# Attention weights used three steps late, and queries and keys of six batches transposed by DMA, in a fused top-k attention and MLP kernel

## The chip, the cores and the metric

The kernel runs on one core of a Trainium2 chip. The metric is the device time of one execution in microseconds; of the kernel before, three runs gave 1605.85, 1606.17 and 1606.31 us, a median of 1606.17 us. The engines are named as the profile names them: PE (TensorE, with PEld for its weight loads), DVE (VectorE), ACT (ScalarE), POOL (GpSimd) and SP (SyncE, which here issues every DMA).

## What is computed

```python
# q, k, v: (8 batches, 8 heads, 576 rows, 64), float32
scores = matmul(q, k^T) / 8
kth    = the 32nd largest score of each row
scores = where(scores >= kth, scores, -1e9)
attn   = exp(scores - rowmax); attn /= (rowsum + 1e-9)
x      = matmul(attn, v), heads side by side: (4608 tokens, 512)
h      = x @ w_in                       # 512 -> 2048
g      = h where h >= 1; 0 where h <= -1; (h + 1)^2 / 4 between
out    = g @ w_out                      # 2048 -> 512
```

## The kernel before

**Steps.** The attention is cut into 144 steps. A step takes 128 query rows against all 576 keys for a pair of heads: four head pairs for each of the four 128-row blocks of a batch, and two steps for the 64 rows that are left over (in these one step serves four heads). Batches go in pairs: 16 steps of the even batch, two and two leftover steps of both, 16 steps of the odd one, so 36 steps a pair. A block of query rows is called a round.

**One step on each engine.** PE multiplies queries and keys (`scores`, tile `sp`, L285), ACT copies the result out (`s`, L287). DVE finds the 32 largest scores (L300 to L386; its first instruction that needs `s` of the next step is L300, tile `more`), ACT takes the exponential (L323), DVE masks and sums (L386), POOL divides (L339). `move_w` (L412) brings the weights into the layout that PE needs without using PE: ACT splits each 32-bit word into its two 16-bit halves (`halves`, L416), SP writes them to DRAM (`rows`, L418), waits, and issues a DMA transpose into `wT` (L419). `values` (L425) then multiplies by V (tile `po`) and ACT copies the product into `xT` (L446). After the last head pair of a block, `mlp` (L457) queues that block's two matrix products, in pieces: eight `ph` groups (L466) and sixteen `py` products (L489), with ACT and POOL between them (L470 to L484).

**Queries and keys** also need a transpose. Before, PE does it against an identity matrix: `queries_of` (L259, tile `pq`, L264) and `keys_of` (L221, tiles `pk` L240 and `pkt` L248), and ACT copies the result out of PSUM (L266, L244, L253). A batch takes 16 + 4 key transposes and 16 + 4 query transposes. The PSUM tiles of `pq`, `pk`, `pkt` and `sp` share one pair of buffers (tag `a`).

**The order** on PE, DVE, ACT and POOL is written out by hand (`manual_schedule`, L580). The loop over steps m (L661) has seven slots; the pieces of DVE's work of step m are given out over the slots, and at the end of each slot `advance` (L562) lets PE take as much queued MLP work as an even share allows (L669 to L673). Within step m, before:

- slot 1: query transposes for step m+3, and in even steps a piece of the next batch's keys
- slot 2: `move_w` of step m-1
- slot 4: scores of step m+2, then `values` of step m-2

SP's order is left to the framework, which sorts it by dependencies. Each of these queues runs strictly in order. For the first steps, until the weights of the MLP have been converted (the variable `early`), another order holds, with transposes of the weights on PE (`transpose_w`).

Of the kernel before, what the change touches and what calls it, by code (L numbers as in the profile page):

```python
# [10 lines left out]
F32 = mybir.dt.float32  # L11
U16 = mybir.dt.uint16
U32 = mybir.dt.uint32
I32 = mybir.dt.int32
AF = mybir.ActivationFunctionType
# [9 lines left out]
def kernel(  # L25
# [10 lines left out]
    nc = tc.nc  # L36
    B, H, S, D = q.shape
    NTOK, DM = out.shape
    DFF = moe_w_in.shape[1]
    P = 128  # L40
# [3 lines left out]
    NHP = H // 2  # L44
    NT = S // P
    SM = NT * P
    TL = S - SM
    assert 2 * TL == P
    SH = S // 2
    BLOCKS = 2 * NT + 1  # L50
# [18 lines left out]
    tiny = const.tile([P, 2], F32, name="tiny")  # L69
# [50 lines left out]
    def load(pool, i, bufs=3):  # L120
        if i < n_pieces and i not in loaded:
            if room and i < 28:
                loaded[i] = room[i % 8]
            else:
                loaded[i] = pool.tile([P, 2 * WC], U32, name="raw", bufs=bufs)
            nc.sync.dma_start(out=loaded[i], in_=pieces_of_weights[i][1].bitcast(U32))

    def words_of(pool, i, bufs=3):
        load(pool, i, bufs)
        words = loaded.pop(i).rearrange("p (n t) -> p n t", t=2)  # L130
        return words[:, :, 0], words[:, :, 1]
# [30 lines left out]

    def inspect_piece(pool, i):

        _, hi = words_of(pool, i, 2)
        for x in range(2):
            sign = pool.tile([P, WC], F32, name="sign", bufs=1)
            nc.scalar.activation(sign, hi.bitcast(F32), AF.Sign, bias=tiny[:, x:x + 1],  # L168
                                 accum_out=signs[:, x, i:i + 1])


    def run(ctx, paired):
# [7 lines left out]
        def whole(x, b):  # L180

            return x[b, :, 0:SM, :].rearrange("h (p c) d -> p h c d", c=NT)
# [38 lines left out]
        def keys_of(b):  # L221
# [14 lines left out]
            for hp in range(NHP):  # L236
# [19 lines left out]
                    got["v"], got["v_tl"] = load_values(b)  # L256
                yield got

        def queries_of(q_in, t, copy=nc.scalar.copy):  # L259
            n = P if t < NT else TL  # L260
            qT = stage.tile([P, NHP, n], F32, name="qT" if t < NT else "qTt")
            pt = ps.tile([P, NHP, n], F32, name="pq", tag="a", bufs=2)
            for hp in range(NHP):
                nc.tensor.transpose(pt[:, hp, :], q_in[:, 2 * hp:2 * hp + 2].rearrange("p j d -> p (j d)"),  # L264
                                    ident[0:n, 0:n])
            copy(qT, pt)  # L266
            return qT
# [62 lines left out]
        def divide(st):  # L330
            rz = att.tile([P, 2], F32, name="rz")
            nc.vector.reciprocal(rz, st["z"])
            if st["by_tensor"]:
                st["rz"] = diag = (late or words).tile([P, 2, P], F32, name="diag", bufs=1)
                for i in range(2):
                    nc.scalar.activation(diag[:, i, :], ident, AF.Copy, scale=rz[:, i:i + 1])
            else:
                for i in range(2):
                    nc.gpsimd.tensor_scalar(st["e"][:, i, :], st["e"][:, i, :], rz[:, i:i + 1], 1.0, ALU.mult, ALU.mult)  # L339
            if paired:  # L340
                m, seconds, kth = st["m"], st["seconds"], st["kth"]
                nc.gpsimd.tensor_tensor(out=excess[:, 2 * m:2 * m + 2], in0=seconds[:, 8:9 + SPLIT:SPLIT], in1=kth[:, LAST:7:-SPLIT],
                                        op=ALU.subtract)
# [50 lines left out]

        def transpose_w(st):
            w = st["e"]
            st["wT"] = wT = (late or words).tile([P, BLOCKS, P], F32, name="wT", bufs=2 if late else 1)
            pt = ps.tile([P, 2, NT, P], F32, name="pw", tag="a", bufs=2)
            for i in range(2):
                for c in range(NT):  # L400
                    nc.tensor.matmul(pt[:, i, c, :], w[:, i, main(i)][:, c * P:(c + 1) * P], st["rz"][:, i, :],  # L401
                                     start=True, stop=True)
            for i in range(2):
                nc.scalar.copy(wT[:, i * (NT + 1):i * (NT + 1) + NT], pt[:, i])
            pt = ps.tile([P, P], F32, name="pwt", tag="a", bufs=2)
            for i in range(2):
                nc.tensor.matmul(pt[i * TL:(i + 1) * TL, :], w[:, i, tail(i)], st["rz"][:, i, :], start=True, stop=True)
            nc.scalar.copy(wT[:, NT], pt)
# [1 line left out]


        def move_w(st):  # L412
            st["wT"] = wT = late.tile([P, BLOCKS, P], F32, name="wT", bufs=2)
            halves = late.tile([P, 2, 2 * S], U16, name="halves")
            for i in range(2):
                nc.scalar.copy(halves[:, :, i * S:(i + 1) * S], st["e"][:, i, :].bitcast(U16).rearrange("p (k t) -> p t k", t=2))  # L416
            rows = dram.tile([P, 2, 2 * S], U16, name="rows")
            nc.sync.dma_start(out=rows, in_=halves)  # L418
            nc.sync.dma_start_transpose(wT.bitcast(U16), rows.rearrange("p t k -> (p t) k"))  # L419
# [37 lines left out]
        def mlp(xT, rows, pool, last):  # L457
# [28 lines left out]
            def final(f):  # L486
                if f == 0:
                    py.append(ps.tile([P, DM], F32, name="py", tag="py", bufs=1))
                nc.tensor.matmul(py[0], gs[f // group][:, f % group], w_out[:, f, :], start=(f == 0), stop=(f == NF - 1))  # L489
                if f == NF - 1:  # L490
                    y = (late or words).tile([P, DM], F32, name="y", bufs=2)
                    nc.scalar.copy(y, py[0])  # L492
                    for p0, p1, dst in rows:
                        nc.sync.dma_start(out=dst, in_=y[p0:p1])
# [111 lines left out]
        def queries(m):  # L606
            nonlocal pe_time
            if m < n and steps[m][0:2] not in qTs:
                r = steps[m][0:2]
                qTs[r] = queries_of(q_ins[r], r[1], nc.vector.tensor_copy if m == 0 else nc.scalar.copy)  # L610
                fetch(rounds.index(r) + 2)
                pe_time += 0.5

        def begin(m):
            b, t, hp, ch, col = steps[m]
# [45 lines left out]
        for m in range(n + 2):  # L661
# [6 lines left out]

            share, left = (total - spent) / (n + 2 - m), sum(x[0] for x in pending)  # L669
            for r in sorted(ready):  # L670
                if r + 3 > m and r >= valued:
                    share = min(share, left / (r + 3 - m))
                    left += NK * NF + NF * DM // P  # L673
            top_k, parts = None, [0] * SLOTS
            if m < n:
# [7 lines left out]
            for slot in range(SLOTS):  # L683
                now = start + (dve_time - start) * (slot + 1) / SLOTS
                for _ in range(parts[slot]):
                    next(top_k, None)
                if m < n and converted < n_pieces:
                    if slot in now_converting:
                        convert(now)
                elif slot == 3 and late is not None:  # L690
                    if m % 2:
                        inspect()
                    elif paired:
                        load(late, inspected, 2)
                if slot == 1 and 1 <= m <= n and state[m - 1]["by_tensor"]:
                    pe_time = max(pe_time, done[m - 1] + 2.0) + 1.0
                    transpose_w(state[m - 1])
                    ready_at[m - 1] = pe_time + 1.8
                if slot == 2 and 1 <= m <= n and not state[m - 1]["by_tensor"]:
                    move_w(state[m - 1])  # L700
                    ready_at[m - 1] = done[m - 1] + 14.0
                if slot == 2 and m == n and paired:
                    judge(ps, att)
                if slot == 2 and (early or m == first_late or m >= n - 1):
                    values_until(m)
                if m == 0 and slot in (1, 2):
                    next(first)
                if slot == 4:
                    begin_at(m + 2)
                    if not early:  # L710
                        values_until(m - 1)
                if slot == (6 if early else 1):
                    queries(m + 3)
                    if m < n and prep is None and next_keys < B and steps[m][0] == next_keys - 1 and steps[m][1] >= 1:
                        prep = keys_of(next_keys)
                    if prep is not None and m % 2 == 0:
                        got = next(prep, None)
                        pe_time += 0.5
                        if got is None:
                            prep, next_keys = None, next_keys + 1  # L720
                        else:
                            keys[next_keys] = got
                advance((EARLY_SHARE if early else share) / SLOTS if m < n else 32.0, now)
# [52 lines left out]
```

## Time and profile before

| quantity | before |
|---|---|
| median of three runs | 1606.17 us |
| the profiled execution's own time | 1610.32 us |
| its span | 1608.5 us |
| DVE busy / ACT busy / POOL busy | 1422.1 / 1140.4 / 943.3 us |
| share of the 16 DMA engines' time taken by SP's queue | 51.8% |
| bytes read from and written to DRAM | 62.91 and 86.11 MB |

Busy time is summed per engine; an engine that is not the bottleneck may idle for free. In a group of instructions the columns are: line, engine, operation, output and inputs, shapes, count, then busy time in us and mean ns of one, then idle time of the engine just before them and what ended it. A row of waits reads: who waited, for whom, us in total, times, longest. The durations of pipelined matmuls overlap: what one costs is the distance from its start to the start of the next.

### The profile page before, as it was taken

The numbers are of one execution on the slowest core, as the hardware profiler recorded it, in microseconds if no ns is written. First come the engines' busy times: TensorE is split into PE (matmuls) and PEld (weight loads), VectorE is DVE, ScalarE is ACT, GpSimd is POOL, SyncE is SP. The second block draws the span as 40 slices with busy tenths as digits, with TensorE's granted clock in tenths as the row PEclk, the third lists the DMA queues.
The fourth block names the chain that finished last, engine by engine and source line by source line (L and its number), as shares of the span: only waits on it lengthen the run. The fifth ranks groups of instructions, "written<-read, shape, count | busy, mean of one in ns | idle before, by whom it ended". The sixth has DMA issues, their size and how long they took to land.

```text
span 1608.5 us, 32395 instructions
## 1 busy us (share of the span) xinstructions
PE 1514.0 (94%) x10925; PEld 1080.7 (67%) x10925; DVE 1422.1 (88%) x4443; ACT 1140.4 (71%) x2308; POOL 943.3 (59%) x1376
## 2 busy tenths in 40 slices
PE   5587999999999999999999999999999999999988
PEld 4465676777667776777667767766666667666665
DVE  7999889999998998999999998999898998889932
ACT  5677567777777767777768877776677776677632
POOL 5766466666555665655556666555555665556640
PEclk7798999999999999999999999999999999999999
DMA  9433246565465556665565545655565555544410
GB/s 252 132 96 110 72 130 174 157 158 153 133 174 161 154 143 173 161 150 145 145 172 159 160 133 157 172 143 140 135 174 146 142 142 130 145 131 126 123 51 16
DMA packets 439056, 227.92 MB, mean 142 GB/s; under 512 B 393056, under 2 KB 401248, under 8 KB 438880
## 3 DMA queue, kind: packets, MB, share of 16 engines
q1 hardware_dynamic: 438880, 225.75, 51.8%
q8 instruction: 88, 1.44, 0.4%
q14 instruction: 88, 0.72, 0.1%
HBM read 62.91 MB, written 86.11 MB: 93 GB/s over the span
## 4 chain that ended last, share of the span: by engine, by line
PE 71%; ACT 13%; POOL 4%; DVE 4%; DMA 4%; issue 3%; SPq 1%; POOLq 0%; ACTq 0%; DVEq 0%
PE ph L466 27%; PE py L489 24%; PE sp L285 8%; PE po L433 7%; ACT halves L416 3%; ACT e L323 3%; DMA wT<-rows 2%; ACT s L287 2%; ACT sign L168 2%; PE pw L401 1%; POOL e L339 1%; POOL r L483 1%; PE po L441 1%; ACT r L470 1%; POOL g L484 1%
## 5 line engine op out<-in xcount | busy, mean ns | idle before, releaser
L466 PEld LDWEIGHTS ph<-xT,w_in 128*128 128x128 f32 x4608 | 554.4, 192 | 118.3 <-issue 79.8
L466 PE MATMUL ph<-xT,w_in 128*128 128x128 f32 x4608 | 576.1, 278 | 14.8 <-ACT xT L446 12.9
L489 PE MATMUL py<-w_out,g 128*128 128x512 f32 x1152 | 558.6, 601 | 7.3 <-ACT y L492 7.1
L482 POOL TENSOR_SCALAR r<-r 128x256 f32<-128x256 f32 x276 | 150.7, 546 | 526.5 <-ACT r L470 526.1
L307 DVE MATCH_REPLACE8 more<-tops,more 128x288 f32<-128x288 f32 x864 | 375.2, 437 | 0.0
L416 ACT COPY halves<-e 128x1152 uint16<-128x1152 uint16 x260 | 288.0, 1153 | 112.7 <-POOL e L339 111.5
L470 ACT ACTIVATE r<-ph,half 128x256 f32<-128x256 f32 (+1 forms) x296 | 139.0, 470 | 241.1 <-PE ph L466 227.9
L489 PEld LDWEIGHTS py<-w_out,g 128*128 128x128 f32 x1152 | 193.5, 191 | 137.0 <-issue 131.2
L386 DVE SCALAR_TENSOR_TENSOR e<-s,kth,e 128x577 f32<-128x577 f32 x288 | 249.2, 900 | 0.1
L484 POOL TENSOR_TENSOR g<-r,g 128x256 f32<-128x256 f32 x280 | 219.6, 784 | 22.0
L323 ACT ACTIVATE e<-s,nmax 128x576 f32<-128x576 f32 x288 | 217.4, 770 | 4.7
L339 POOL TENSOR_SCALAR e<-e,rz 128x576 f32<-128x576 f32 x260 | 218.6, 851 | 0.0
L483 POOL TENSOR_TENSOR r<-r 128x256 f32<-128x256 f32 x276 | 201.5, 730 | 23.0
L300 DVE TENSOR_TENSOR more<-s 128x576 f32<-128x576 f32 x144 | 114.9, 798 | 109.0 <-ACT s L287 108.6
L287 ACT ACTIVATE s<-sp 128x576 f32<-128x576 f32 x288 | 169.2, 638 | 4.5 <-PE sp L285 4.2
L285 PE MATMUL sp<-kT,qT 64*128 64x288 f32 x1024 | 162.0, 433 | 9.9 <-ACT kT L244 9.0
L285 PEld LDWEIGHTS sp<-kT,qT 64*128 64x128 f32 x1024 | 89.6, 188 | 98.9 <-issue 29.1
L433 PE MATMUL po<-wT,v_in 128*64 128x128 f32 x2048 | 145.9, 282 | 10.3 <-DMA wT<-rows 7.9
L433 PEld LDWEIGHTS po<-wT,v_in 128*64 128x64 f32 x2048 | 113.4, 139 | 60.5 <-issue 37.5
L477 ACT ACTIVATE g<-ph,minus 128x256 f32<-128x256 f32 x280 | 131.8, 471 | 0.0
L348 DVE MAX8 tops<-more 128x8 f32<-128x288 f32 x288 | 125.4, 442 | 0.0
L300 DVE TENSOR_TENSOR less<-s 128x576 f32<-128x576 f32 x144 | 117.4, 815 | 0.0
(92 smaller groups left out, 1528.2 us busy)
## 6 DMA issues: line engine op xcount, KB each, us to landing
rows<-halves SPq DMA_DIRECT2D x130, 576.0 KB, 2.8
raw<-in_moe_w_out_dram SPq DMA_DIRECT2D x52, 256.0 KB, 2.8
raw<-in_moe_w_in_dram SPq DMA_DIRECT2D x48, 256.0 KB, 2.9
k_in<-in_k_dram SPq DMA_DIRECT2D x64, 128.0 KB, 3.2
q_in<-in_q_dram SPq DMA_DIRECT2D x32, 256.0 KB, 3.3
v_in<-in_v_dram SPq DMA_DIRECT2D x8, 1024.0 KB, 5.9
out_dram<-y SPq DMA_DIRECT2D x32, 256.0 KB, 3.0
kT<-in_moe_w_in_dram SPq DMA_DIRECT2D x16, 256.0 KB, 4.6
```

The lines of the kernel that those rows point to most:

```text
L285: nc.tensor.matmul(o[:, a0 - c0:a1 - c0], qT[d, g, :], kT[d, g, k0:k0 + a1 - a0], start=True, stop=True)
L300: nc.vector.tensor_tensor(out=x, in0=s[:, :, 0:SH], in1=s[:, :, SH:S], op=op)
L307: nc.vector.match_replace(out=st["rest"][:, i, :], in_to_replace=eight(st["tops"], i, r - 8), in_values=src[:, i, :], imm_value=LOWEST)
L323: nc.scalar.activation(e[:, i, :], s[:, i, :], AF.Exp, bias=nmax[:, i:i + 1])
L339: nc.gpsimd.tensor_scalar(st["e"][:, i, :], st["e"][:, i, :], rz[:, i:i + 1], 1.0, ALU.mult, ALU.mult)
L386: nc.vector.scalar_tensor_tensor(out=st["all"][1][:, i, :], in0=st["all"][0][:, i, :], scalar=last[i], in1=st["all"][1][:, i, :], op0=ALU. ...
L416: nc.scalar.copy(halves[:, :, i * S:(i + 1) * S], st["e"][:, i, :].bitcast(U16).rearrange("p (k t) -> p t k", t=2))
L433: nc.tensor.matmul(po[j * D:(j + 1) * D], v_in[:, h, c, :] if c < NT else v_tl[0][:, h, :], wT[:, block(j, c)], start=(c == 0), stop=(c == ...
L466: nc.tensor.matmul(ph[:, i], w_in[:, kk, f * P:(f + 1) * P], xT[:, kk], start=(kk == 0), stop=(kk == NK - 1))
L483: nc.gpsimd.tensor_tensor(out=r, in0=r, in1=r, op=ALU.mult)
L484: nc.gpsimd.tensor_tensor(out=g, in0=r, in1=g, op=ALU.add)
L489: nc.tensor.matmul(py[0], gs[f // group][:, f % group], w_out[:, f, :], start=(f == 0), stop=(f == NF - 1))
```

## The change

- `values` runs for step m-3 instead of m-2, in slot 2 instead of slot 4, ahead of the scores of step m+2, which also move from slot 4 to slot 2. `move_w` goes from slot 2 to slot 3. `wT` gets a third buffer; `advance` counts with the later supply of MLP work (`r + 4`).
- Queries and keys of batches 3 to 8 are no longer transposed by PE. `turn` does with them what `move_w` does with the weights: an ACT copy into 16-bit halves, a DMA to DRAM, a DMA transpose. For this the keys are loaded in blocks of 128 rows of all heads (`load_block`, with three DMAs a block) and not by head pair. Slots stay as they were; the last two blocks of a batch's keys (c = 3 and 4) are turned in the same slot. The buffer `parts` of the halves exists once.
- To make room, the tile for the MLP's output `y` and the buffer of the weights' inspection (`raw`) go from two to one, and `diag` shares a tag with `halves`.

```diff
+        def turn(x, dst):
+            n = x.shape[0]
+            parts = stage.tile([P, 2, H * D], U16, name="parts", tag="k_tl", bufs=1)[0:n]
+            nc.scalar.copy(parts, x.rearrange("p h d -> p (h d)").bitcast(U16).rearrange("p (k t) -> p t k", t=2))
+            lines = dram.tile([P, 2, H * D], U16, name="lines")[0:n]
+            nc.sync.dma_start(out=lines, in_=parts)
+            nc.sync.dma_start_transpose(dst.bitcast(U16), lines.rearrange("p t k -> (p t) k"))
+
+        def turned_keys_of(b):
...
+            blocks = {0: load_block(0)}
+            yield got
+            for c in range(NT + 1):
+                if c < NT:
+                    blocks[c + 1] = load_block(c + 1)
+                n = P if c < NT else TL
+                turn(blocks.pop(c)[0:n], kT[:, :, c * P:c * P + n])
+                if c == NT - 2:
+                    got["v"], got["v_tl"] = load_values(b)
+                if c != NT - 1:
+                    yield got
+
+        def turned_queries_of(q_in, t):
+            n = P if t < NT else TL
+            qT = stage.tile([P, NHP, n], F32, name="qT" if t < NT else "qTt")
+            turn(q_in, qT)
+            return qT
...
-            st["wT"] = wT = late.tile([P, BLOCKS, P], F32, name="wT", bufs=2)
+            st["wT"] = wT = late.tile([P, BLOCKS, P], F32, name="wT", bufs=3)
...
-                    y = (late or words).tile([P, DM], F32, name="y", bufs=2)
+                    y = (late or words).tile([P, DM], F32, name="y", bufs=1)
...
-                qTs[r] = queries_of(q_ins[r], r[1], nc.vector.tensor_copy if m == 0 else nc.scalar.copy)
+                if r[0] > 1:
+                    qTs[r] = turned_queries_of(q_ins[r], r[1])
+                else:
+                    qTs[r] = queries_of(q_ins[r], r[1], nc.vector.tensor_copy if m == 0 else nc.scalar.copy)
+                    pe_time += 0.5
                 fetch(rounds.index(r) + 2)
-                pe_time += 0.5
...
-                if r + 3 > m and r >= valued:
-                    share = min(share, left / (r + 3 - m))
+                if r + 4 > m and r >= valued:
+                    share = min(share, left / (r + 4 - m))
...
-                if slot == 2 and 1 <= m <= n and not state[m - 1]["by_tensor"]:
+                if slot == 3 and 1 <= m <= n and state[m - 1] is not None and not state[m - 1]["by_tensor"]:
                     move_w(state[m - 1])
-                    ready_at[m - 1] = done[m - 1] + 14.0
+                    ready_at[m - 1] = done[m - 1] + 15.0
...
-                if slot == 4:
+                if slot == 2 and not early:
+                    values_until(m - 2)
+                if slot == (4 if early else 2):
                     begin_at(m + 2)
-                    if not early:
-                        values_until(m - 1)
...
-                        prep = keys_of(next_keys)
+                        prep = (turned_keys_of if next_keys > 1 else keys_of)(next_keys)
```

More of the change, by code (lines that the diff above doesn't have):

```diff
@@ L163, in inspect_piece @@
     def inspect_piece(pool, i):
-        _, hi = words_of(pool, i, 2)
+        lo, hi = words_of(pool, i, 1)
         for x in range(2):
-            sign = pool.tile([P, WC], F32, name="sign", bufs=1)
-            nc.scalar.activation(sign, hi.bitcast(F32), AF.Sign, bias=tiny[:, x:x + 1],
+            nc.scalar.activation(lo.bitcast(F32), hi.bitcast(F32), AF.Sign, bias=tiny[:, x:x + 1],
                                  accum_out=signs[:, x, i:i + 1])
@@ L257, in keys_of, with load_block @@
                 yield got
+        def turn(x, dst):
[6 more added lines that the diff above has]
+        def turned_keys_of(b):
+            kT = stage.tile([P, NHP, S], F32, name="kT")
+            got = dict(kT=kT)
+            def load_block(c):
+                x = stage.tile([P, H, D], F32, name="k_block", tag="k_in")
+                ends = k[b, :, SM:S, :].rearrange("h p d -> p h d")
+                if c < NT:
+                    nc.sync.dma_start(out=x[:, 0::2, :], in_=whole(k, b)[:, 0::2, c, :])
+                    nc.sync.dma_start(out=x[TL:P, 1::2, :], in_=whole(k, b)[0:P - TL, 1::2, c, :])
+                else:
+                    nc.sync.dma_start(out=x[0:TL, 0::2, :], in_=ends[:, 0::2, :])
+                nc.sync.dma_start(out=x[0:TL, 1::2, :], in_=whole(k, b)[P - TL:P, 1::2, c - 1, :] if c else ends[:, 1::2, :])
+                return x
+            blocks = {0: load_block(0)}
+            yield got
+            for c in range(NT + 1):
+                if c < NT:
+                    blocks[c + 1] = load_block(c + 1)
[10 more added lines that the diff above has]
+            return qT
         def queries_of(q_in, t, copy=nc.scalar.copy):
@@ L333, in divide @@
             if st["by_tensor"]:
-                st["rz"] = diag = (late or words).tile([P, 2, P], F32, name="diag", bufs=1)
+                st["rz"] = diag = (late or words).tile([P, 2, P], F32, name="diag", tag="halves", bufs=1)
                 for i in range(2):
@@ L396, in transpose_w @@
             w = st["e"]
-            st["wT"] = wT = (late or words).tile([P, BLOCKS, P], F32, name="wT", bufs=2 if late else 1)
+            st["wT"] = wT = (late or words).tile([P, BLOCKS, P], F32, name="wT", bufs=3 if late else 1)
             pt = ps.tile([P, 2, NT, P], F32, name="pw", tag="a", bufs=2)
@@ L609, in queries @@
                 r = steps[m][0:2]
-                qTs[r] = queries_of(q_ins[r], r[1], nc.vector.tensor_copy if m == 0 else nc.scalar.copy)
+                if r[0] > 1:
+                    qTs[r] = turned_queries_of(q_ins[r], r[1])
+                else:
+                    qTs[r] = queries_of(q_ins[r], r[1], nc.vector.tensor_copy if m == 0 else nc.scalar.copy)
+                    pe_time += 0.5
                 fetch(rounds.index(r) + 2)
-                pe_time += 0.5
         def begin(m):
@@ L693, in run @@
                     elif paired:
-                        load(late, inspected, 2)
+                        load(late, inspected, 1)
                 if slot == 1 and 1 <= m <= n and state[m - 1]["by_tensor"]:
@@ L714, in run @@
                     if m < n and prep is None and next_keys < B and steps[m][0] == next_keys - 1 and steps[m][1] >= 1:
-                        prep = keys_of(next_keys)
+                        prep = (turned_keys_of if next_keys > 1 else keys_of)(next_keys)
                     if prep is not None and m % 2 == 0:
                         got = next(prep, None)
-                        pe_time += 0.5
+                        pe_time += 0.5 if next_keys < 2 else 0.0
                         if got is None:
```

## The prediction

> **What bounds the kernel now.** I read the page's engine table and its slices first, then the busy time of the even stretch from 200 to 1500 us.
>
> ```profile
> PE 1514.0 (94%) x10925; PEld 1080.7 (67%) x10925; DVE 1422.1 (88%) x4443; ACT 1140.4 (71%) x2308; POOL 943.3 (59%) x1376
> ...
> PE   5587999999999999999999999999999999999988
> ...
> PEclk7798999999999999999999999999999999999999
> ```
>
> ```profile
> 200.00:1500.00 1300.00, 1271.45 (x9359) 901.07 (x9358) 1195.72 (x3750) 956.63 (x1883) 785.60 (x1137) 1.00 0.56 150
> ```
>
> The columns of the second are PE, PEld, DVE, ACT and POOL busy, the granted clock, the DMA share and GB/s. From 200 us on PE is busy 97.8% at full clock, DVE 92.0%. The 250 masking instructions (L386, two a step) in this stretch make 125 steps, so a step takes 10.40 us, of which DVE is busy 9.57. A busy PE may still hide slack, so I looked at its instructions in order of time, in a step that nothing disturbs and in one with a query transpose:
>
> ```profile
> 1197.39 1.24 PE L285 MATMUL sp<-kT,qT 64*128 64x288 f32 x8
> 1198.56 1.09 PE L433 MATMUL po<-wT,v_in 128*64 128x128 f32 x16
> 1199.49 0.39 PE L433 MATMUL po<-wT,v_tail 128*64 128x128 f32 x4
> 1199.81 2.05 PE L466 MATMUL ph<-xT,w_in 128*128 128x128 f32 x16
> 1201.69 1.88 PE L489 MATMUL py<-w_out,g 128*128 128x512 f32 x4
> 1203.41 1.95 PE L466 MATMUL ph<-xT,w_in 128*128 128x128 f32 x16
> 1205.20 1.88 PE L489 MATMUL py<-w_out,g 128*128 128x512 f32 x4
> 1207.01 1.24 PE L285 MATMUL sp<-kT,qT 64*128 64x288 f32 x8
> ...
> 1223.49 0.60 PE L264 MATMUL pq<-ident,q_in 128*128 128x128 f32 x4
> 1223.93 1.95 PE L466 MATMUL ph<-xT,w_in 128*128 128x128 f32 x16
> ```
>
> Each burst starts before the one ahead of it has ended: 1207.01 - 1197.39 = 9.62 us for a plain step with no gap at all. That is above DVE's 9.57. So PE bounds, by a little, and DVE follows. The waits agree: DVE stands for `s`, which PE makes, while PE stands for little:
>
> ```profile
> DVE more L300 <- ACT s L287: 108.6, 89, 4.9
> ...
> PE ph L466 <- ACT xT L446: 12.9, 10, 2.2
> ...
> PE po L433 <- DMA wT<-rows: 7.9, 6, 3.5
> ```
>
> The Trainium skill speaks against this reading: its page "Perfetto Trace Analysis", section "Identifying the Most-Contended Engine", says that matmul busy time misleads because matmuls are pipelined, and that the share of weight loading should be used. By that share (67%) PE would have a third to spare, and taking work from it would be worth nothing. The gapless starts above say otherwise, and the sum goes by them.
>
> **The change, part by part.**
>
> *Transposes off PE.* A batch has 32 of 128 columns and 8 of 64. Four of the former cost 1223.93 - 1223.49 = 0.44 us from start to start, 0.11 each; for the latter I take 0.10 at most. Six batches: 6 x (32 x 0.11 + 8 x 0.10) = 26 us off PE. The busy times of these rows give an upper bound:
>
> ```profile
> L240 PE MATMUL pk<-ident,k_in 128*128 128x128 f32 x128 | 20.7, 289 | 5.8 <-ACT s L287 5.0 <-ACT wT L404 0.8
> L264 PE MATMUL pq<-ident,q_in 128*128 128x128 f32 x128 | 19.4, 274 | 3.6 <-ACT s L287 2.8 <-DVE kT L244 0.8
> ```
>
> With 3.9 and 3.7 us for the leftover rows, 47.7 x 6/8 = 36 us; the difference is each burst's end, which lies under the next burst. The built instruction lists show the same: priced by start-to-start distances, PE's work falls by 25.5 us. **-26.**
>
> *Values one step later and ahead of the scores.* `wT` gets 5 slots (0.71 of a 10.4 us step, 7.4 us) more time. The waits of `po` for it in this stretch and its end are 7.9 (L433) and 2.1 (L441) us; one of 2.55 us at the very end stays. **-8** (0 to -10). The waits of `ph` for `xT`, 12.9 + 1.9 us, are those of a new block's first product for the last `values`; now a scores burst of 1.17 us (1197.39 to 1198.56) stands between, against a mean wait of 1.3 us. **-10** (0 to -15).
>
> *ACT.* Sixty turns add as many copies. The nearest row is `halves`:
>
> ```profile
> L416 ACT COPY halves<-e 128x1152 uint16<-128x1152 uint16 x260 | 288.0, 1153 | 112.7 <-POOL e L339 111.5
> ```
>
> 1024 of 1152 columns make 1.03 us, 62 us in all. The copies out of PSUM that go are 8 x 0.578 + 2 x 0.366 + 4 x 0.587 + 0.373 = 8.1 us a batch, 48 us. ACT gains 13 us where it idles 343 of 1300: nothing by itself. But `parts` exists once: when blocks 3 and 4 of the keys are turned in one slot, ACT's second copy waits until the first has been written out, 0.34 us of issue and the 2.8 us of `rows` below. Behind it on ACT stand `xT`, `s`, and the `r` and `g` that free PE's `ph` buffers (three). PE has a `py` burst (1.72 us) or two to go on with. Six times 0 to 3.1 us; near the low end because of that cover: **+4** (0 to 19).
>
> *SP and the DMA engines.* SP gains 60 writes, 60 transposes and 30 key loads. What it issues for the weights:
>
> ```profile
> rows<-halves SPq DMA_DIRECT2D x130, 576.0 KB, 2.8
> ...
> wT<-rows SPq DMA_TRANSPOSE x130, 4.7
> ```
>
> In SP's built order a turn's write and transpose stand between the weights' own. A query turn, issued in slot 1 of step m, is needed by scores in slot 2 of step m+1: one step and a `po` burst later, 9.6 + 1.2 = 10.8 us. Its chain: copy 1.03, issue 0.34, landing 2.8, transpose 4.7 at the size of `wT` or 2.1 at 4/9 of it: 6.3 to 8.9 us, and 2.6 more when a `wT` transpose is ahead of it, 11.5. Thirty query turns lose 0 to 0.7 us: **+2** (0 to 21). Keys have four steps or more: nothing. The DMA engines take 0.56 of their time; the turns add 9 full-size equivalents of 256 KB to 18 of 576 KB per batch, 22%, so 0.68: no queue by bytes. `y` with one buffer is written four steps apart and lands in 3.0: nothing. Were this cover gone, each of these waits would stand ahead of the scores, because `values` and scores are now adjacent.
>
> The Trainium skill, page "VectorE: DVE Perf Modes", section "Rules for kernel authors", advises TensorE for a 128x128 transpose wherever a PSUM destination will do, and the DMA crossbar only otherwise; here PSUM does. By that rule the -26 would turn into a loss. The rows above decide: the time on PE is on the path, that on the DMA engines is not.
>
> *End.* The built lists show 8 `ph` and 8 `py` steps of work (twice as many matmuls: 16 x 0.112 + 16 x 0.429 = 8.7 us) moved from the loop to behind the last scores, because `advance` rations by `r + 4`. It is the same PE work, and costs nothing while PE bounds the loop; where DVE sets the pace, up to 8.7. **+3.**
>
> **Sum:** -26 - 8 - 10 + 4 + 2 + 3 = -35 us. The profiled execution of 1610.3 us (span 1608.5) would become 1575; the runs' median lies 4.1 lower, so 1571. Per step: 10.40 - 35/125 = 10.12, still above DVE's 9.57.
>
> **Rivals.**
>
> *More of the waits go* (0.14). DVE's 108.6 us for `s` shrink because scores come two slots earlier (3 us), and PE, no longer disturbed, comes near its gapless 9.62 to 9.8 us a step: 125 x 0.4 = 50 us and more. 1548 to 1558. For it: undisturbed steps already run gapless; against it: PE and DVE are too close to run without stalls.
>
> *Lockstep* (0.18). With PE's step at 9.6 and DVE's at 9.57 any jitter stops one or the other, and half to all of the 26 us come back as waits of PE: -35 + 13 to 26 is -22 to -9, and with the end at its full 8.7 (6 more) -16 to -3: 1584 to 1603, the upper fifth of which cannot be told from before. For it: the two engines' steps differ by 0.05 us; against it: a step has slack on both sides, three `s` tiles and scores that now come two slots earlier.
>
> *Late queries: slower* (0.16). The mechanism is SP's strict order: a turn's transpose waits for its write to land, and behind it stand the weights' writes, which free `halves`, for which ACT waits. In the trace a `wT` transpose took up to 8.8 us to land, when V was being loaded. If every query turn holds PE up by more than 35/30 = 1.2 us, nothing is gained; at 2.5 us each it costs 75 - 35 = +40: 1646. For it: SP already spends 0.34 + 2.8 + 2.56 = 5.7 us of each step on `rows`, its landing and the issue of `wT` (2.56 is the median time that this issue holds SP), and a turn adds 0.34 + 1.1 + up to 2.8. Against it: 10.8 us of time for a chain of 6.3 to 8.9.
>
> *The forecast* (0.52): 1558 to 1588.
>
> **Numbers.** This kernel's measurement can tell 0.2% (3.2 us) from no change. Faster: 0.52 + 0.14 + 0.14 = 0.80; same 0.04; slower 0.16. The range takes in the first three cases, 1548 to 1604, and leaves out the slower one.
>
> **What would show it.** Right: steps of about 10.1 us; no `pq`, `pk` after the first two batches; waits of `po` for `wT` and of `ph` for `xT` nearly gone; DVE's wait for `s` well below 100 us; PE's span after DVE's last mask longer. Wrong: PE's waits named by the transposes into `qT`; ACT idle before `parts` by more than 19 us; SP standing for landings with `halves` waiting behind. If DVE's wait for `s` grows while PE idles, the late queries have decided.

## The result and the profile after

The changed kernel took 1583.05 us (median of four runs, 1578.63 to 1585.57) against 1606.24 us of the kernel before in the same comparison: a ratio of 0.9848 (95% interval 0.9821 to 0.9875), or -23.2 us. The profiled execution was the fastest of the four, 1578.63 us (span 1576.8), 31.7 us below that of before.

The engine table, the busy slices and the granted clock of the profile after:

```profile
PE 1481.3 (94%) x10685; PEld 1056.7 (67%) x10685; DVE 1432.2 (91%) x4443; ACT 1162.1 (74%) x2278; POOL 939.0 (60%) x1376
...
PE   5587899999999999999999999999999999999998
...
PEclk6799999999999999999999999999999999999999
```

The stretch from 200 to 1500 us, with the columns of the prediction:

```profile
200.00:1500.00 1300.00, 1269.75 (x9307) 898.82 (x9306) 1237.07 (x3855) 1002.08 (x1897) 800.78 (x1164) 1.00 0.67 176
```

PE is 32.7 us less busy in all, yet its share of the span is unchanged at 94%: the span shrank with it. DVE went from 92.0 to 95.2% of the stretch. The stretch now holds 128 steps instead of 125, so a step takes 10.16 us instead of 10.40. A plain step, from one `po` burst to the next, is 1207.43 - 1197.82 = 9.61 us, as before (9.62): the gain lies in the steps that are not plain. The end grew: from DVE's last masking to the end of the span it is 74.2 us, against 68.5.

The waits of the whole execution after (who, for whom, us, times, longest; line numbers are those of each kernel, so the L300 and L287 of before are the L342 and L329 here):

```profile
DVE more L342 <- ACT s L329: 39.6, 34, 4.3
DVE e L428 <- ACT e L365: 22.5, 23, 1.8
PE py L531 <- ACT y L534: 19.6, 13, 2.8
ACT parts L262 <- DMA lines<-parts: 14.7, 5, 4.5
...
PE po L475 <- DMA wT<-rows: 5.2, 4, 1.7
PE po L483 <- ACT parts L262: 3.8, 2, 1.9
PE ph L508 <- ACT xT L488: 2.6, 1, 2.6
...
ACT halves L458 <- POOL e L381: 1.1, 3, 0.5
```

DVE's wait for `s` fell from 108.6 to 39.6 us, and ACT's for POOL's division ahead of `halves` from 111.5 to 1.1. PE's waits for `xT` fell from 14.8 to 2.6. In their place PE waits for `y` (19.6, before 7.1), and DVE for an exponential (22.5, new). Summed over `po`, `ph` and `py`, PE waits as long as before: 10.0 + 14.8 + 7.1 = 31.9, then 7.2 + 3.8 + 2.6 + 19.6 = 33.2.

Who was late with `s` is told by ACT's copies that make it, before and after:

```profile
L287 ACT ACTIVATE s<-sp 128x576 f32<-128x576 f32 x288 | 169.2, 638 | 4.5 <-PE sp L285 4.2
```

```profile
L329 ACT ACTIVATE s<-sp 128x576 f32<-128x576 f32 x288 | 173.3, 647 | 67.8 <-PE sp L327 63.8
```

Before, ACT waited 4.2 us in all for PE's scores: they lay ready, and ACT came late to copy them. After, ACT waits 63.8 us for them: it is there before they are. So hardly any of DVE's 108.6 us for `s` before was a wait for PE.

### The profile page after: what moved, and what is told of

The parts are those of the page before. It is cut to its first block, busy times and chain, and to the rows that moved or that the text cites. A ratio compares the mean times of both kernels' runs of the same rounds, so it can differ in the third digit from the quotient of the medians.

```text
span 1576.8 us, 32399 instructions
## 1 busy us (share of the span) xinstructions
PE 1481.3 (94%) x10685; PEld 1056.7 (67%) x10685; DVE 1432.2 (91%) x4443; ACT 1162.1 (74%) x2278; POOL 939.0 (60%) x1376
## 4 chain that ended last, share of the span: by engine, by line
PE 79%; ACT 8%; DMA 5%; DVE 4%; issue 2%; POOL 1%; ACTq 0%; DVEq 0%; POOLq 0%; SPq 0%
PE ph L508 29%; PE py L531 28%; PE sp L327 10%; PE po L475 9%; ACT halves L458 2%; DMA rows<-halves 2%; DMA wT<-rows 2%; PE pw L443 1%; PE po L483 1%; ACT e L365 1%; DVE bits L147 1%; DMA lines<-parts 1%; DVE more L349 1%; ACT s L329 1%; ACT r L512 1%
## 5 line engine op out<-in xcount | busy, mean ns | idle before, releaser
L531 PE MATMUL py<-w_out,g 128*128 128x512 f32 x1152 | 556.2, 601 | 19.6 <-ACT y L534 19.6
L524 POOL TENSOR_SCALAR r<-r 128x256 f32<-128x256 f32 x276 | 144.1, 522 | 500.1 <-ACT r L512 500.0
L428 DVE SCALAR_TENSOR_TENSOR e<-s,kth,e 128x577 f32<-128x577 f32 x288 | 263.9, 945 | 23.0 <-ACT e L365 22.5
L526 POOL TENSOR_TENSOR g<-r,g 128x256 f32<-128x256 f32 x280 | 228.4, 816 | 22.0
L365 ACT ACTIVATE e<-s,nmax 128x576 f32<-128x576 f32 x288 | 222.5, 773 | 4.7
L381 POOL TENSOR_SCALAR e<-e,rz 128x576 f32<-128x576 f32 x260 | 226.0, 878 | 0.0
L329 ACT ACTIVATE s<-sp 128x576 f32<-128x576 f32 x288 | 173.3, 647 | 67.8 <-PE sp L327 63.8
L525 POOL TENSOR_TENSOR r<-r 128x256 f32<-128x256 f32 x276 | 197.2, 714 | 23.0
L475 PEld LDWEIGHTS po<-wT,v_in 128*64 128x64 f32 x2048 | 112.3, 138 | 77.7 <-issue 17.9
L342 DVE TENSOR_TENSOR more<-s 128x576 f32<-128x576 f32 x144 | 114.4, 794 | 40.1 <-ACT s L329 39.6
L342 DVE TENSOR_TENSOR less<-s 128x576 f32<-128x576 f32 x144 | 118.9, 826 | 0.0
```

The costliest lines, as they stand in the source:

```text
L342: nc.vector.tensor_tensor(out=x, in0=s[:, :, 0:SH], in1=s[:, :, SH:S], op=op)
L365: nc.scalar.activation(e[:, i, :], s[:, i, :], AF.Exp, bias=nmax[:, i:i + 1])
L428: nc.vector.scalar_tensor_tensor(out=st["all"][1][:, i, :], in0=st["all"][0][:, i, :], scalar=last[i], in1=st["all"][1][:, i, :], op0=ALU. ...
L475: nc.tensor.matmul(po[j * D:(j + 1) * D], v_in[:, h, c, :] if c < NT else v_tl[0][:, h, :], wT[:, block(j, c)], start=(c == 0), stop=(c == ...
L525: nc.gpsimd.tensor_tensor(out=r, in0=r, in1=r, op=ALU.mult)
L526: nc.gpsimd.tensor_tensor(out=g, in0=r, in1=g, op=ALU.add)
```

## The experiments

The kernel before had a median of 1607.69 us beside the first four experiments, 1609.34 beside the next four and 1610.28 beside the last four. Ratios are to these. Between the groups this base moved by 2.6 us, so two kernels of different groups that lie a few us apart are not told apart.

### One part alone, and the double turn taken away

**e1_turns_only**: the kernel before, with the new functions `turn`, `turned_keys_of` and `turned_queries_of` of the diff, and of the schedule this (its own estimates of PE's time, `pe_time`, follow suit and are left out here):

```diff
-                qTs[r] = queries_of(...)
+                if r[0] > 1:
+                    qTs[r] = turned_queries_of(q_ins[r], r[1])
...
-                        prep = keys_of(next_keys)
+                        prep = (turned_keys_of if next_keys > 1 else keys_of)(next_keys)
```

> The kernel before with the turns alone: queries and keys of batches 3 to 8 go through DMA, values and scores keep their old slots and lag. My theory (PE bounds, and its 26 us of transposes are on the path): 1584 to 1592, which is 1606 - 26 plus 6 x 2.6 us for the double key turns at most. The rival (the reorder brings all of the gain, and what the turns save on PE they cost on ACT and SP): 1604 to 1612, with more waits of po for wT than the 10 us of before, because wT still has only two steps.

1632.13 us (1627.55 to 1636.49), 1.0142 (1.0119 to 1.0165): **24 us slower**, outside what either theory expected, though the waits for `wT` that the rival named did grow. Its waits:

```profile
DVE more L343 <- ACT s L330: 138.5, 87, 5.6
ACT halves L459 <- POOL e L382: 128.9, 61, 3.2
PE po L476 <- DMA wT<-rows: 24.7, 19, 4.1
PE ph L509 <- ACT xT L489: 20.9, 12, 2.6
```

The weights come late: PE's wait for `wT` rose from 10.0 to 31.4 us (24.7 and 6.7 for the leftover rows), for `xT` from 14.8 to 23.1. The six double turns are in this kernel too (ACT stands 14.9 us ahead of `parts`); what they add here was not taken apart. A second loss follows from the first. PE's instructions in order of time after one of these waits, and the row of the granted clock (the last but two) for the same place:

```profile
336.55 1.24 PE L328 MATMUL sp<-kT,qT 64*128 64x288 f32 x8
341.82 1.98 PE L476 MATMUL po<-wT,v_in 128*64 128x128 f32 x16 [4.04 <-DMA wT<-rows]
343.56 0.67 PE L476 MATMUL po<-wT,v_tail 128*64 128x128 f32 x4
344.15 3.78 PE L509 MATMUL ph<-xT,w_in 128*128 128x128 f32 x16
```

```profile
341.00:345.00 4.00, 3.18 (x24) 2.88 (x25) 4.00 (x16) 3.94 (x11) 1.35 (x2) 0.53 0.52 184
```

After an idle of 4.04 us the same burst of `ph` takes 3.78 us instead of the 2.05 of a plain step, at half clock. From 200 to 1500 us such stretches add up to 47.8 us in e1, against 3.4 us before and 3.4 us after the change; half of it, some 24 us, is lost. So PE's 25.5 us less work are outweighed by 35.5 us more of waits (all that stand at `po`, `ph` and `py`: 33.8 to 69.3) and 22 us of slower clock: +32, of which the profiled execution shows +26.2 (1636.49 against 1610.32).

**e2_order_only**: the changed kernel, with all transposes on PE.

```diff
-                if r[0] > 1:
+                if r[0] >= B:
...
-                        prep = (turned_keys_of if next_keys > 1 else keys_of)(next_keys)
+                        prep = (turned_keys_of if next_keys >= B else keys_of)(next_keys)
```

> The changed kernel with all queries and keys transposed by PE as before, so that only the order (values three steps late and ahead of the scores, the halves in slot 3, three wT buffers, one y) is new. My theory: 1589 to 1597, 1606 less the 18 us of waits for wT and xT plus up to 8 us for the y copy that now stands behind the halves on ACT. The rival (the order alone brings the gain): 1578 to 1584, no slower than the changed kernel.

1583.64 us (1582.42 to 1585.35), 0.9846 (0.9829 to 0.9864): the change's own time, as the rival had it. **The order alone gives the whole gain.**

```profile
DVE more L342 <- ACT s L329: 37.7, 34, 3.3
DVE e L428 <- ACT e L365: 26.6, 27, 1.8
PE py L531 <- ACT y L534: 12.3, 11, 2.5
...
PE po L475 <- DMA wT<-rows: 1.7, 2, 1.1
```

PE's waits for `wT`, `xT` and `y` fall from 31.9 to 14.0 us; none for `xT` is left. As much PE work as before, and 24 us less time: the turns, as they stand in the change, are worth nothing. The traces say where most of their 25.5 us went: in the change the same waits of PE, with the one behind `parts`, are 33.2 us, 19.2 more than here.

**e3_one_turn_a_slot**: the changed kernel, with blocks 3 and 4 of the keys in slots of their own.

```diff
-                if c != NT - 1:
-                    yield got
+                yield got
```

> The changed kernel with the fifth key block turned two steps after the fourth and not in the same slot. My theory (ACT standing for the single parts buffer holds up y, xT and s, and these hold up PE): the 17 us of ACT's wait before parts vanish and the time falls by 6 x 2 to 6 x 2.8, to 1566 to 1572. The rival (PE has other work to run meanwhile, and ACT catches up): 1580 to 1585, no change.

1569.33 us (1566.65 to 1571.86), 0.9751 (0.9732 to 0.9770): 13.7 us below the change, as the first theory had it, and the fastest kernel of this study that computes everything. ACT no longer waits ahead of `parts`; PE's waits for `wT`, `xT` and `y` are 24.5 us. The double turn thus costs 13.7 us between the medians, 2.3 us for each of its six times; the two profiled executions, the fastest of the change and the slowest of e3, lie 6.8 us apart. Against e2 the turns, one a slot, bring 14.3 of their 25.5 us. About as much as is missing comes back as waits of PE, 10.5 us more than in e2, 9.8 of them for `wT` (11.5 against 1.7). One double turn in the trace of the change, ACT and PE in order of time (lines between are left out):

```profile
1276.01 1.04 ACT L262 COPY parts<-k_block 128x1024 uint16<-128x1024 uint16 x1
...
1280.16 1.04 ACT L262 COPY parts<-k_block 64x1024 uint16<-64x1024 uint16 x1 [3.12 <-DMA lines<-parts]
1281.11 0.57 ACT L534 COPY y<-py 128x512 f32<-128x512 f32 x1
...
1281.83 1.96 PE L531 MATMUL py<-w_out,g 128*128 128x512 f32 x4 [2.60 <-ACT y L534]
```

ACT stands 3.12 us until the first of the two blocks has been written out of `parts`; the copy of `y` that frees PE's next `py` buffer stands behind it, and PE stands 2.60 us.

**e4_keys_only**: the changed kernel with the queries on PE (`if r[0] >= B:` in the place of `if r[0] > 1:`).

> The changed kernel with queries transposed by PE again, keys by DMA. My theory (each batch's query transposes cost PE half of the 26 us): 13 us slower than the changed kernel less what 30 fewer turns relieve on SP, 1590 to 1597. The rival (the query turns' latency on SP costs as much as PE saves): 1578 to 1586.

1589.08 us (1588.08 to 1590.20), 0.9877 (0.9858 to 0.9897): 6 us above the change, between the two expectations, and 5.4 us above e2, which turns nothing: the turns of the keys, double ones included, are a loss. The six double turns remain (14.3 us of ACT's waits ahead of `parts`), while PE has the query transposes back. No query turn delays the scores in the change: PE's wait for `qT` is 0.2 us, once.

### The DMA transpose taken away

Four kernels replace each DMA transpose by a plain copy of the same bytes. The transposition is left out in them. They ask what it costs that a transpose's issue holds SP and that it lands later.

```diff
-            nc.sync.dma_start_transpose(wT.bitcast(U16), rows.rearrange("p t k -> (p t) k"))
+            nc.sync.dma_start(out=wT.bitcast(U16), in_=rows.rearrange("p t k -> p (t k)").rearrange("p (b c) -> p b c", b=BLOCKS))
```

**c1_copy_before** (the kernel before with this edit), **c2_copy_turns_spread** (c1 with the turns, one a slot, in the old order), **c3_copy_order** (the new order, transposes of queries and keys on PE), **c4_copy_order_turns** (the new order with the turns, one a slot).

> The kernel before, with every DMA transpose replaced by a plain DMA copy of the same bytes from the same DRAM tile into the same destination; the transposition is what it leaves out, so it computes on untransposed weights. It is the first corner of a square: old or new order, PE transposes or turns, all without the DMA transpose's hold on SP (2.56 us of issue per step) and its later landing. Both theories: the 10 us of waits of po for wT go, 1592 to 1600.

> As the first, plus the turns (as plain copies too, so queries and keys of batches 3 to 8 are not transposed either), the fifth key block two steps after the fourth; old order. With real DMA transposes and double turns this took 1632. My theory (turns lose in the old order because DMA transposes fill SP and the DMA engines until wT is late, and each long stall of PE is followed by half clock): without them wT is early, and the 25 us of PE work come off the first corner: 1568 to 1577. The rival (ACT's order and the lockstep with DVE eat the gain, not SP): 1588 to 1598, no better than the first corner.

> As the first corner, with the new order and PE transposes for queries and keys. With real transposes this took 1584 and po waited 1.1 us for wT. Both theories: nothing left to gain from an earlier wT, 1580 to 1586.

> The fourth corner: new order and turns, one key turn a slot, all transposes as plain copies. With real transposes this took 1569, 14 less than the order alone where 25 us of PE work had gone. My theory (the other 11 us are po's waits for a late wT, 10.9 us there): 1555 to 1562. The rival (with PE's work cut, DVE sets the pace, and the rest of the 25 us cannot show): 1565 to 1571.

| | median us | ratio (95%) |
|---|---|---|
| c1 | 1653.38 | 1.0275 (1.0249 to 1.0300) |
| c2 | 1652.70 | 1.0263 (1.0239 to 1.0286) |
| c3 | 1597.07 | 0.9918 (0.9897 to 0.9939) |
| c4 | 1569.56 | 0.9743 (0.9722 to 0.9765) |

c1 and c3 missed what both theories expected, by an unmeant edit: to give the copy whole rows, `halves` was written with a stride, and that made ACT's copy longer, 0.35 us each, 0.7 us a step. The same copy is in c2 and c4, and in their turns: c2 falls outside both expectations, and c4, though in its rival's range, has a load that neither theory counted. The group of `halves` in c1, and then in d1 below, where the stride is gone:

```profile
L416 ACT COPY halves<-e 128x1152 uint16<-128x1152 uint16 x260 | 372.2, 1500 | 144.4 <-POOL e L339 143.8
```

```profile
L416 ACT COPY halves<-e 128x1152 uint16<-128x1152 uint16 x260 | 287.9, 1154 | 113.0 <-POOL e L339 112.1
```

The longer copy made the best test of the study. Within the square, all four corners with it, the turns gain nothing in the old order (c2 against c1: -0.7 us): PE's 25.5 us come back as 20 us more waits in the stretch from 200 to 1500 us (49.5 to 69.7) and 58.0 us at half clock there instead of 20.5. In the new order they gain 27.5 us (c4 against c3), all of the work taken off PE. c4 is no faster than e3, though hardly any wait for `wT` (1.9 us) is left in it; but it carries the longer copies, which alone cost 13.7 us in the new order (d2 below), so this does not say what the late weights cost in e3.

### The dose, and what is left

**d1_copy_before_lean** and **d2_copy_order_lean** are c1 and c3 with the copy at its old length.

```diff
-                nc.scalar.copy(halves.rearrange("p t k -> p (t k)")[:, i * 2 * S:(i + 1) * 2 * S].rearrange("p (k t) -> p t k", t=2),
-                               st["e"][:, i, :].bitcast(U16).rearrange("p (k t) -> p t k", t=2))
+                nc.scalar.copy(halves.rearrange("p t k -> p (t k)")[:, i * 2 * S:(i + 1) * 2 * S], st["e"][:, i, :].bitcast(U16))
```

> The first corner of the square again (the kernel before, DMA transposes replaced by plain copies of the same bytes, transposition left out), but the copy into halves contiguous on both sides. In the first version that copy had a strided output and took 1.50 us instead of 1.15, and the kernel took 1653. Theory A (in the old order ACT is in the loop, because halves wait for POOL and stand ahead of s, so 0.7 us more of ACT a step cost 44 us): with the copy at 1.15 us or less 1595 to 1606. Theory B (the plain copies themselves disturb, ACT does not matter): 1640 to 1655.

1602.82 us (1600.34 to 1605.92), 0.9958 (0.9945 to 0.9972), as Theory A had it. The plain copies are worth 7.5 us in the old order; they leave 5.4 of the 10.0 us of PE's waits for `wT`. And 0.7 us of ACT a step, 91 us over 130 steps, cost 1653.38 - 1602.82 = 51 us there, though ACT is busy only 71% in the kernel before.

> The third corner (new order, PE transposes, plain copies) with the contiguous copy into halves; the strided one took 1597, the kernel with real DMA transposes 1584. Theory A: 1577 to 1585, so the 0.7 us of ACT cost 12 to 20 here, a third of what they cost in the old order. Theory B: 1593 to 1600.

1583.38 us (1582.65 to 1583.99), 0.9843 (0.9827 to 0.9860), Theory A again, and equal to e2: in the new order without turns a DMA transpose costs nothing that shows, and the same dose costs 1597.07 - 1583.38 = 13.7 us.

**d3_copy_halves_later**: c4 with `move_w` in slot 4 instead of 3, which puts the second exponential ahead of `halves`.

```diff
-                if slot == 3 and 1 <= m <= n and state[m - 1] is not None and not state[m - 1]["by_tensor"]:
+                if slot == 4 and 1 <= m <= n and state[m - 1] is not None and not state[m - 1]["by_tensor"]:
```

> The fourth corner (new order, turns one a slot, plain copies, strided halves, 1570) with move_w in slot 4 instead of 3, behind the second exponential. My theory (DVE's 32 us of waits for the exponential and PE's 17 us for y are both of the halves standing ahead on ACT, and both engines have 9.6 us a step to do): 1548 to 1562. The rival (one of the two engines has slack for its wait, and the halves now delay something else): 1565 to 1573.

1565.70 us (1563.53 to 1567.48), 0.9727 (0.9708 to 0.9747): 3.9 us below c4, which was measured in another group; the ratios' intervals overlap. DVE's wait for the exponential, 32.1 us in c4, is gone from the list, and its wait for `s` rose from 26.8:

```profile
DVE more L343 <- ACT s L330: 47.9, 44, 4.3
PE py L533 <- ACT y L536: 15.7, 8, 3.1
```

The waits change their names and the time hardly moves, as the rival had it. That fits two engines that both pace, with plain steps of 9.6 us on PE and DVE nearly as busy, but no run shows it apart from other causes.

**d4_copy_ration_r3**: c4 with the ration of MLP work as before.

```diff
-                if r + 4 > m and r >= valued:
-                    share = min(share, left / (r + 4 - m))
+                if r + 3 > m and r >= valued:
+                    share = min(share, left / (r + 3 - m))
```

> The fourth corner (1570) with the MLP work rationed by r + 3 as in the kernel before. My theory (8.7 us of PE work behind the last scores cost about 3): 1563 to 1568. The rival (PE's work costs the same inside the loop): 1567 to 1573, slower if the queue of MLP work runs empty.

1580.63 us (1579.68 to 1585.32), 0.9823 (0.9806 to 0.9839): 11 us slower than c4. PE's wait for `y` rose from 20.4 to 27.8 us, with single waits of up to 4.8. The trace has most of the loss at the end: from DVE's last masking to the end it is 82.0 us, against 72.0 in c4, with 240 matmuls of `ph` and 80 of `py` there instead of 224 and 70. So the old ration leaves more work for the end, not less. The likely reading is that the queue of MLP work runs empty before the later `values` fills it; that is argued, not shown.

## Why the prediction was right, and where it was not

The time fell, and it landed in the forecast's band (1558 to 1588), 12 us above its 1571. The sum behind it was made of parts that the runs split otherwise: order -24 and turns 0, where it said -18 and -17 with the end. That the time still fell within the band is in part luck: the order gave 6 us more than its terms, and the band is wide enough to miss the turns' 17.

- **"PE bounds, by a little."** True of plain steps, which are gapless before and after at 9.6 us. What failed is the reading of DVE's wait. The prediction let `s` be late because PE makes it, and gave ACT "nothing by itself"; but PE's scores lay ready (4.2 us of ACT's waits), and ACT's queue was late. In the old order `halves` waits on ACT for POOL (111.5 us), and the `s` that DVE wants (108.6 us) and the `xT` that PE wants stand behind it. The doses show that this queue reaches the time: 51 us for 91 us on an engine that idles a quarter of the time, and 13.7 in the new order. How much of the order's 24 us came this way is not shown: PE's waits for `wT`, `xT` and `y` account for 17.9, near the 18 that the sum has for the first two.
- **Transposes off PE, -26.** PE's work did fall so far, but it became time only where the rest could follow: +24 us with the turns alone (e1), -0.7 in the old order with plain copies (c2), and, against the new order without turns, 0 in the change, -14 in e3 and -27.5 with plain copies (c4). What the term is worth hangs on the order around it and on the double turn.
- **`wT` -8.** Sized right for the order alone: its waits fell from 10.0 to 1.7 us. In the change 7.2 us of them stand, so the turns bring them back; that their writes and transposes between the weights' own on SP do it is argued. The five slots were counted to `values`; the copies into `halves` also moved one slot later, so four are left for the way through DRAM, 5.9 us of a 10.4 us step.
- **`xT` -10.** Its waits fell from 14.8 to 2.6 us, and to none with the order alone.
- **The double turn, +4 (0 to 19).** Measured 13.7 between the medians, within its bounds, mis-sized. It listed `xT`, `s`, `r` and `g` behind the waiting copy, and not the copy of `y`, which frees PE's buffer first. ACT stood 16.9 us ahead of `parts`, less than the 19 named as the mark of an error.
- **Late queries, +2, and the slower rival.** Not so: 0.2 us. A turn's write lands in 2.6 us and its transpose in 3.3, inside the 10.8 us it has.
- **End, +3.** The tail did grow by 5.7 us. But the term was charged to `r + 4`, and with `r + 3` and the later values the kernel is 11 us slower and its tail 10 us longer (d4): there the sign was wrong.
- **Not foreseen:** DVE's new wait for the second exponential. `halves`, two copies, 2.19 us, now stands ahead of it on ACT. With that wait gone (d3) 3.9 us are won at most. Also PE's wait for `y`, put at nothing: with the order alone it rose from 7.1 to 12.3 us.
- **Rivals.** Lockstep, priced at 1584 to 1603, begins 1 us above the measured median, so the time alone does not tell it from the forecast. Its jitter between PE and DVE is not what most of the trace shows: what comes back in e3 is mostly PE's wait for `wT`, and in the change the waits behind the double turn.

The Trainium skill (page "VectorE: DVE Perf Modes", section "Rules for kernel authors") prefers TensorE for such transposes. e1 shows a loss of 24 us, e3 against e2 a gain of 14, but these differ in the order and in the double turn; c1 to c4 differ in the order alone and show 0.7 us of gain and 27.5. So the runs decide it by the order around the transposes, which the rule does not ask for.

Left open: the turns one a slot in the old order with real transposes, values three steps late without standing ahead of the scores, e3 with the later `halves` or with `r + 3`, and c4 with the short copy were not tried. Nor was the new order taken apart: later halves, earlier scores and later values came together, and which of them frees ACT is open. A ledger of PE's work, named waits and clock comes out 6 to 9 us above the difference of the profiled executions in e1, e2, e3 and the change; that remainder has not been broken down.

## What to carry to other kernels

In a queue that runs strictly in order, ask of each instruction that waits what stands behind it: an engine busy 71% can hold up the loop, and adding a small dose to it tells so at once. A row of waits names who came last; ask the engine in between whether its own input lay ready. Test the parts of an edit one by one and in each other's company; here one part was worth 0.7 or 27.5 us by the order around it alone (c1 to c4), and a loss of 24 as it was first tried alone. A single buffer used twice in one slot is a wait for a DMA's landing, on every instruction behind it.

## What the runs showed of the hardware

- PE's clock halves after short idles too. Stretches of 3.4 or 6.8 us at half clock began within a few us of idles of 1.9 to 4.1 us, though not after every one: in the trace before, an idle of 3.52 us had none, one of 1.86 us had (traces before and e1, from 200 us on). The Trainium skill (page "TensorE: Matmul & The Clock Gate", section "Why this matters for your kernels") asks for no gaps above about 3 us; some of the gaps found here are shorter. Its section "What's actually happening" gives a window of about 3.4 us, with which the lengths of the stretches agree.
- ACT's copy of 128x1152 16-bit values took 1.50 us with input and output strided (c1) and 1.15 us with only the input strided (before) or with both contiguous (d1). A strided output alone was not measured.
- In the change, a transpose of 256 KB landed 3.3 us after its issue and held SP for 1.25 us; one of 576 KB landed in 4.9 and held it for 2.56. A plain copy of the same 576 KB landed in 3.9 (d2) and held SP for 0.32 (c1, d1). All are medians.
